# Training step of two attention and two GLU layers: one GLU slope product fused on VectorE, a scale delayed by one chunk, and query and slope loaded apart in attention backward

## The chip, the cores and the metric

The kernel runs on one core of a Trainium2 chip. Its engines are TensorE (PE in the profile, with PEld for its weight loads), VectorE (DVE), ScalarE (ACT), GpSimd (POOL) and SyncE (SP, which mainly issues transfers). Each engine executes its own instructions in order; semaphores tie the engines together. The metric is the device time of one execution in microseconds (us), and the median over several runs is compared.

## The reference

The input x is 2048 tokens by 512 features, in bf16. Two kinds of layer are applied twice in turn, A, B, A, B, each to the layer norm of x and added to x. Then the gradients with respect to x and all weights are taken for a given output gradient.

```python
def A(x, wqkv, wo):                      # 32 heads of 16 features
    q, k, v = heads(x @ wqkv)
    phi = lambda t: where(t > 0, t + 1, exp(t)) + 1e-6
    pq, pk = phi(q), phi(k)
    kv, z = einsum("bhsd,bhse->bhde", pk, v), einsum("bhsd->bhd", pk)
    num = einsum("bhqd,bhde->bhqe", pq, kv)
    den = einsum("bhqd,bhd->bhq", pq, z)[..., None] + 1e-6
    return merge(num / den) @ wo

def B(x, w_gate, w_up, w_down):          # 512 -> 1376 -> 512
    return (sigmoid(x @ w_gate) * (x @ w_up)) @ w_down

x = x + A(layernorm(x)); x = x + B(layernorm(x))
x = x + A(layernorm(x)); x = x + B(layernorm(x))
# outputs: x, and d(x . grad_out) / d(A_x, wqkv, wo, w_gate, w_up, w_down)
```

The B layers are called GLU layers here. Both A layers share their weights, and so do both B layers.

## The kernel before, in words

The layers are numbered 0 to 3; 0 and 2 are attention, 1 and 3 GLU. The 2048 tokens are cut into NBLK = 4 blocks of SB = 512, each of NB = 4 tiles of 128; the 512 features into NDC = 4 chunks, and the 1376 GLU features into NFC = 11 chunks of 128 (the last overlaps). The kernel is written with a tile framework: tiles come from pools with a fixed number of buffers, the framework sets the waits and moves instructions within each engine's order by its own estimate, so the order of the source is only approximately the order on an engine. Parts of different layers are generators that are stepped in turn, which interleaves their work.

`glu` (L635) makes one chunk of one block: four matmuls each for g and u into two PSUM banks. With t = tanh(-g/2), ScalarE leaves t in place of g (L647) and writes 1 - t into half 0 of the tile sd (L648); VectorE makes hh = (1 - t) u / 2 (L649), the activated value; ScalarE writes 1 + t into half 1 (L650), and GpSimd multiplies that by hh (L651). Half 1 is then the slope that the gradient of g needs, half 0 that of u.

The time line of the profiled execution:

- to 112 us: attention layer 0 and the first block of GLU layer 1;
- 112 to 215 us: forward of GLU layer 1 (`b_fwd`), interleaved with the second half of layer 0 (L532, L535, L546: den, its reciprocal, the output products). Each block's `down` (L675) multiplies hh by the down weights and adds to x (L428), and then asks for the layer norm of that block for layer 2 (`nxt.need`): per two tiles two ACT squares (L299), POOL's L301 and L302, two DVE operations L304, and a DMA transpose (L307); per block a store (L310). hh and sd are stored by SP for the backward.
- 215 to 524 us: attention layer 2, then forward and backward of GLU layer 3 in one pass (`b_both`, from 267 us). For each chunk: `glu`, then dhh = the down weights' transpose by the gradient (four matmuls, ACT L732), then VectorE's one multiplication of both slopes by dhh (L733, "scale"), in place, and the stores of the result: in block 0 by `store_dd`, afterwards by a DMA transpose in `turn_dd`. In its first block the second half of layer 2 runs between. `dh_b` (L790) makes the gradient of the block's normed input. The transposed gate and up weights wgT and wuT are loaded during this stage by `load_b_bwd`: a big transposing transfer (L418), a small one (L419), and a GpSimd memset of the unused rows (L420).
- 524 to 574 us: first backward half of attention layer 2 (`a_bwd1`); the same for layer 0 from 766 to 813 us. Per block SP loads `qr` (query and slope together, 1024 KB, tag "sh" with 2 buffers) and qn (512 KB). Per chunk: dq (PE L180, copied by ACT L1005), u = dq times query (DVE L1007), a sum over heads (PE L977, t_ps), w (DVE L979, tile w_t with 2 buffers), dqT = w times slope (POOL L980), and a product for the normaliser (DVE L981). `k.fill.step` inserts matmuls of weight gradients between.
- 574 to 640 us second half of that layer; 640 to 766 us the backward of GLU layer 1 (`b_bwd`, L868, L885); 766 to 880 us attention layer 0; from 880 us the weight gradients (L1199, L1217).

In the forward 8 PSUM banks serve the tag "bank", in the backward 4.

Of the kernel before, what the change touches and what calls it, by code (L numbers as in the profile page):

```python
# [7 lines left out]
BF16 = mybir.dt.bfloat16  # L8
F32 = mybir.dt.float32
ACT = mybir.ActivationFunctionType  # L10
ALU = mybir.AluOpType
# [620 lines left out]
                yield True  # L632


def glu(k, hT, fc):  # L635

    nc = k.nc
    g_ps = k.ps.tile([P, SB], F32, name="g_ps", tag="bank")
    mm4(k, g_ps[:], lambda c: k.wg[:, c, FC0[fc]:FC0[fc] + P], lambda c: hT[:, :, c, :])
    u_ps = k.ps.tile([P, SB], F32, name="u_ps", tag="bank")  # L640
    mm4(k, u_ps[:], lambda c: k.wu[:, c, FC0[fc]:FC0[fc] + P], lambda c: hT[:, :, c, :])
    hh = k.p_hh.tile([P, SB], BF16, name="hh_t")
    if k.n_sd % 2 == 0:
        k.sd2 = k.p_sd.tile([P, 2, 2, SB], BF16, name="sd_t", tag="sd")
    sd = k.sd2[:, k.n_sd % 2]
    k.n_sd += 1
    nc.scalar.activation(g_ps[:], g_ps[:], ACT.Tanh, scale=-0.5)  # L647
    nc.scalar.activation(sd[:, 0, :], g_ps[:], ACT.Identity, bias=k.onef[:], scale=-1.0)  # L648
    nc.vector.scalar_tensor_tensor(hh[:], sd[:, 0, :], 0.5, u_ps[:], ALU.mult, ALU.mult)  # L649
    nc.scalar.activation(sd[:, 1, :], g_ps[:], ACT.Identity, bias=k.onef[:])  # L650
    nc.gpsimd.tensor_tensor(sd[:, 1, :], sd[:, 1, :], hh[:], ALU.mult)  # L651
    return hh, sd


# [5 lines left out]
def b_fwd(k, l, ln, nxt):  # L660
    nc, sv = k.nc, k.sv[l]
    hhs, late = {}, []

    def store():

        b, fc, hh, sd = late.pop()
        store_hh(k, sv, b, fc, hh, nc.sync)
        nc.sync.dma_start(out=sv["sd"][b, fc], in_=sd.rearrange("p a b -> p (a b)"))

    def down(b):  # L670
        ys = [k.ps.tile([P, D], F32, name="y_ps", tag="bank") for _ in range(NB)]
        for fcs in (range(NFC - 1), (NFC - 1,)):
            for j in range(NB):
                for fc in fcs:
                    nc.tensor.matmul(ys[j][:], lhsT=hhs[b][fc][:, rows(j)], rhs=k.wd[:, fc, :],  # L675
                                     start=(fc == 0), stop=(fc == NFC - 1))
        for j in range(NB):
            add_x(k, b * NB + j, ys[j])
        nxt.need(b * NB + NB - 1)

    for b in range(NBLK):
        hhs[b] = []
        if b:
            down(b - 1)
        for fc in range(NFC):
            hh, sd = glu(k, ln.hT[b], fc)
            hhs[b].append(hh)
            if late:
                store()
            late.append((b, fc, hh, sd))  # L690
            yield b, fc
    store()
    down(NBLK - 1)


def last_grads(k, b):
# [7 lines left out]
def b_both(k, l, ln, ctx):  # L704

    nc, sv = k.nc, k.sv[l]
    pool = lambda name, bufs: ctx.enter_context(k.tc.tile_pool(name=name, bufs=bufs))
    hhs, dds, gns, gTs = {}, {}, k.gns, k.gTs
    k.n_t, k.fused = 2, lambda st: True

    def down(b):
        for j in range(NB):
            st = b * NB + j
            y_ps = k.ps.tile([P, D], F32, name="y_ps", tag="bank")
            mm4(k, y_ps[:], lambda fc: hhs[b][fc][:, rows(j)], lambda fc: k.wd[:, fc, :], NFC)
            if j % 2 == 0:
                ost = k.p_o.tile([P, 2, D], BF16, name="o0_t")
            nc.vector.tensor_tensor(ost[:, j % 2, :], y_ps[:], k.xs[st][:], ALU.add)
            if j % 2:
                k.st.dma_start(out=by_tile(k.out0, st - 1, 2), in_=ost[:])  # L720

    for b in range(NBLK):
        ln.need(b * NB + NB - 1)
        hhs[b], dds[b] = [], []
        if b == 1:
            k.p_ln, k.p_o, k.p_nat = pool("ln3", 2), pool("o3", 2), pool("nat", 2)
        for fc in range(NFC):
# [5 lines left out]
            k.last_mul = nc.vector.tensor_tensor(dd, dhh[:].unsqueeze(1).to_broadcast([P, 2, SB]), dd, ALU.mult)  # L733
            hhs[b].append(hh)
            dds[b].append(dd)
            if b:
                turn_dd(k, sv, b, fc, dd)
            else:
                store_dd(k, sv, b, fc, dd, nc.sync)
            store_hh(k, sv, b, fc, hh, k.st)  # L740
            if fc == 1 and b:
                down(b - 1)
                dh_b(k, l, b - 1, dds[b - 1], ln.h[b - 1], gns[b - 1])
            if fc == 3 and b + 1 < NBLK:
                last_grads(k, b + 1)
                if b:
                    ln.need((b + 2) * NB - 1)
            if b == NBLK - 1 and fc == 5:
                k.early = a_grads(k, 0)
            yield b, fc  # L750
    b = NBLK - 1
    down(b)
    dh_b(k, l, b, dds[b], ln.h[b], gns[b])
    flush_nat(k)


def turn_dd(k, sv, b, fc, dd):

    i, f = divmod(fc, 4)
    p0 = FDUP if fc == NFC - 1 else 0  # L760
    if f == 0:
        k.nat = k.p_nat.tile([P, 2, NB, D], BF16, name="nat_t")
    k.nc.sync.dma_start_transpose(
        out=k.nat[:, :, :, f * P - p0:(f + 1) * P - p0].rearrange("p a j f -> p (a j) f"),
        in_=dd.rearrange("p a s -> p (a s)"))
    if f == 1:
        flush_nat(k)
    if f == 3 or fc == NFC - 1:
        w = SETS[i][1]
        k.nats.append((sv["ddN"][b, i, :, :, :, 0:w], k.nat[:, :, :, 0:w]))  # L770
# [190 lines left out]
def a_bwd1(k, l, big, ph1, p_dq):  # L961
# [2 lines left out]
    nc.sync.dma_start(out=flat(MT), in_=sv["MT"][:])  # L964
    dzp = big.tile([P, NDC, NBLK], F32, name="dzp")
    CT_ps = [k.ps2.tile([P, D], F32, name="CT_ps", tag="dwbank") for _ in range(NDC)]
    late, gs, dqTs = [], [k.early], []

    def sums(b, g_t, qn):
        for jc in range(NDC):  # L970
# [1 line left out]
                nc.tensor.matmul(CT_ps[jc][:], lhsT=g_t[:, j, jc * P:(jc + 1) * P], rhs=qn[:, :, j, :],  # L972
                                 start=(b == 0 and j == 0), stop=(b == NBLK - 1 and j == NB - 1))

    def soft(b, dc, dq, u_t, qp, rp, dqT):
        t_ps = k.ps.tile([P, SB], F32, name="t_ps", tag="bank")
        nc.tensor.matmul(t_ps[:], lhsT=k.bdmask[:], rhs=u_t[:], start=True, stop=True)  # L977
        w_t = ph1.tile([P, SB], BF16, name="w_t")
        nc.vector.scalar_tensor_tensor(w_t[:], t_ps[:], A["nz"][:, dc:dc + 1], dq[:], ALU.mult, ALU.add)  # L979
        nc.gpsimd.tensor_tensor(dqT[:, dc, :], w_t[:], rp[:, dc, :], ALU.mult)  # L980
        nc.vector.scalar_tensor_tensor(u_t[:], t_ps[:], -1.0, qp[:, dc, :], ALU.mult, ALU.mult,  # L981
                                       accum_out=dzp[:, dc, b:b + 1])
        if dc == NDC - 1:
            k.st.dma_start(out=by_chunk(sv["dqT"], b), in_=dqT[:])

    k.fill.step(12)
    for b in range(NBLK):
        g_t, gT = gs[b]
        qr = k.p_sh.tile([P, 2, NDC, SB], BF16, name="qr_l", tag="sh")
        qp, rp = qr[:, 0], qr[:, 1]  # L990
        nc.sync.dma_start(out=flat(qr), in_=sv["qr"][b])
        qn = k.p_h.tile([P, NDC, NB, P], BF16, name="qn_l", tag="h_t")
        nc.sync.dma_start(out=flat(qn), in_=sv["qn"][b])
        if b == 1 and l == 2:
            nc.sync.dma_start_transpose(out=k.woT[:], in_=k.w_in["wo"])
            nc.sync.dma_start_transpose(out=k.wqkvT[:], in_=k.w_in["wqkv"])
        if b == NBLK - 1 and l == 2:
            held(k, k.mark, nc.sync.dma_start_transpose(out=k.wdT[:], in_=k.w_in["wd"]))
        dqT = p_dq.tile([P, NDC, SB], BF16, name="dqT_t")
        dqTs.append(dqT)  # L1000
        for dc in range(NDC):
            ps = k.ps.tile([P, SB], F32, name="dq_ps", tag="bank")
            mm4(k, ps[:], lambda c: MT[:, c, dc * P:(dc + 1) * P], lambda c: gT[:, :, c, :])
            dq = ph1.tile([P, SB], BF16, name="dq_sb", bufs=3)
            k.mark = nc.scalar.copy(dq[:], ps[:])  # L1005
            u_t = ph1.tile([P, SB], BF16, name="u_t", bufs=3)
            nc.vector.tensor_tensor(u_t[:], dq[:], qp[:, dc, :], ALU.mult)  # L1007
            late.append((b, dc, dq, u_t, qp, rp, dqT))
            k.fill.step(2)
            if len(late) > 2:  # L1010
                soft(*late.pop(0))
            if dc in (0, 2) and b + 1 < NBLK:
                g = a_grads(k, b + 1, dc // 2)
                if dc:
                    gs.append(g)
        sums(b, g_t, qn)
    while late:
        soft(*late.pop(0))
# [236 lines left out]
```

## Time and profile before

| | |
|---|---|
| median of 13 runs | 1136.6 us |
| lowest and highest | 1131.16 and 1143.16 us |
| the profiled execution | 1131.92 us, of which the span 1130.0 us |
| mean granted TensorE clock | 0.994 |
| PE busy | 1079.6 us (96%) |
| DVE, ACT, POOL busy | 528.1, 487.5, 325.9 us |
| loads of query and slope | 8 of 1024 KB, 7.2 us from issue to landing |
| loads of qn | 8 of 512 KB, 4.8 us |

How to read the lines of the profile: a group line names the source line, engine, operation, output and inputs, shape and count; then the busy time and mean length of one, and the idle time just before, with what ended it. A line of the time line gives start and length in us, and in square brackets how long the engine stood idle before and which instruction released it. The rows by stretch give for each engine its busy time and number of instructions, then the granted TensorE clock (1.00 is full speed), the mean busy share of the 16 DMA engines (waiting transfers can take it over 1), and GB/s.

### The profile page before, as it was taken

The page shows a single profiled execution, that of the slowest core. Times are in us where ns is not written, and L with a number is a line of the kernel's source. Part 1 is how long each engine was busy: PE and PEld are TensorE (multiplying, and loading weights), DVE is VectorE, ACT ScalarE, POOL GpSimd, SP SyncE. Part 2 cuts the span into 40 slices and gives each one's busy share as a digit, 9 for nine tenths or more (in the row PEclk, how much of TensorE's full clock was granted, in tenths as well). Part 3 has the DMA queues.
Part 4 walks back from the last instruction along what each step waited for, and adds up shares of the span by engine and source line. Part 5 has one row for each costly group of instructions (what it writes and reads, how often), then busy time and mean ns, then how long its engine had stood idle before and what let it go on. Part 6 is the DMA issues. An engine that isn't in the chain of part 4 may idle for free.

```text
span 1130.0 us, 15668 instructions
## 1 busy us (share of the span) xinstructions
PE 1079.6 (96%) x5624; PEld 509.2 (45%) x5624; DVE 528.1 (47%) x983; ACT 487.5 (43%) x1002; POOL 325.9 (29%) x427
## 2 busy tenths in 40 slices
PE   6989999998899999999899999999999999999898
PEld 3444444444334444444444444444444444464343
DVE  7685755667734445434657624556667100000100
ACT  3476877547635546453425533335436100000011
POOL 5424655303632526141442200003513200001110
PEclk9999999999999999999999999999999999999899
DMA  9977988679993939399995898859973797689995
GB/s 263 270 226 238 261 235 246 189 181 239 289 224 85 247 82 238 90 248 279 231 333 167 222 272 232 242 169 310 346 198 101 181 281 175 145 184 256 251 226 133
DMA packets 376558, 248.12 MB, mean 220 GB/s; under 512 B 288785, under 2 KB 341041, under 8 KB 374689
## 3 DMA queue, kind: packets, MB, share of 16 engines
q1 hardware_dynamic: 361424, 197.73, 70.3%
q0 software_dynamic: 15056, 49.39, 12.7%
q8 instruction: 44, 0.72, 0.3%
q14 instruction: 34, 0.27, 0.1%
HBM read 74.48 MB, written 102.20 MB: 156 GB/s over the span
## 4 chain that ended last, share of the span: by engine, by line
PE 26%; issue 20%; POOL 4%; DMA 3%; DVE 2%; ACT 1%; POOLq 0%; DVEq 0%; ACTq 0%
PE dh_ps L885 7%; PE dhh_ps L180 3%; PE fill_ps L236 3%; PE dw_ps L1199 2%; PE CT_ps L972 2%; PE dh_ps L790 2%; PE dq_ps L180 2%; PE dh_ps L1107 2%; PE dh_ps L1046 2%; DMA qr_l<-sv_qr 1%; POOL out_dram L1127 1%; PE dpk_ps L180 1%; POOL x L865 1%; PE y_ps L180 1%; DMA hf_t<-sv_hhT 1%
## 5 line engine op out<-in xcount | busy, mean ns | idle before, releaser
L1199 PE MATMUL dw_ps<-set_t,h_all 128*128 128x512 bf16 (+1 forms) x1024 | 204.8, 362 | 2.0 <-ACT dw_new L1126 2.0
L1199 PEld LDWEIGHTS <-h_all 128*128 128x128 bf16 x1024 | 100.1, 98 | 106.0 <-issue 2.6
L651 POOL TENSOR_TENSOR sd_t<-sd_t,hh_t 128x512 bf16<-128x512 bf16 x88 | 106.6, 1220 | 120.0 <-DVE hh_t L649 89.2
L1126 ACT CAST dw_new<-dw_ps 128x512 bf16<-128x512 f32 (+1 forms) x40 | 19.8, 572 | 220.7 <-PE dw_ps L1199 156.2
L855 ACT ACTIVATE t_sb<-dh_ps,rstd 128x512 f32<-128x512 f32 x64 | 43.5, 680 | 131.6 <-PE dh_ps L790 94.9
L180 PE MATMUL g_ps<-hT_t,wg 128*128 128x512 bf16 x352 | 90.5, 379 | 6.9 <-DVE hh_t L649 3.7
L1223 DVE TENSOR_TENSOR dw_new<-dw_ps,part_l 128x512 bf16<-128x512 f32 (+1 forms) x11 | 7.2, 687 | 181.2 <-PE dw_ps L1217 168.5
L180 PE MATMUL u_ps<-hT_t,wu 128*128 128x512 bf16 x352 | 90.5, 379 | 0.6 <-DVE hh_t L649 0.6
L180 PE MATMUL dhh_ps<-gT_t,wdT 128*128 128x512 bf16 x352 | 90.3, 379 | 0.0
L885 PE MATMUL dh_ps<-wgT,dd_t 128*128 128x512 bf16 x176 | 66.7, 379 | 0.0
L885 PE MATMUL dh_ps<-wuT,dd_t 128*128 128x512 bf16 x176 | 66.7, 379 | 0.0
L649 DVE SCALAR_TENSOR_TENSOR hh_t<-sd_t,u_ps 128x512 bf16<-128x512 bf16 x88 | 59.2, 678 | 14.1 <-ACT sd_t L648 13.5
L1127 POOL DMA_DIRECT2D out_dram<-dw_new x36 | 19.3, 541 | 151.6 <-ACT dw_new L1126 150.2
L648 ACT ACTIVATE sd_t<-g_ps,onef 128x512 bf16<-128x512 f32 x88 | 60.8, 690 | 2.5
L650 ACT ACTIVATE sd_t<-g_ps,onef 128x512 bf16<-128x512 f32 x88 | 60.6, 688 | 0.0
L733 DVE TENSOR_TENSOR sd_t<-dhh_t,sd_t 128x1024 bf16<-128x1024 bf16 x44 | 30.4, 692 | 61.4 <-POOL sd_t L651 60.0
L908 DVE TENSOR_TENSOR dd_t<-dhh_t,sh_t 128x1024 bf16<-128x1024 bf16 x44 | 29.9, 689 | 58.6 <-ACT dhh_t L906 48.3
L647 ACT ACTIVATE g_ps<-g_ps 128x512 f32<-128x512 f32 x88 | 52.4, 602 | 8.8 <-PE g_ps L180 8.7
L180 PEld LDWEIGHTS <-wg 128*128 128x128 bf16 x352 | 33.9, 98 | 47.1 <-issue 8.8
L180 PEld LDWEIGHTS <-wu 128*128 128x128 bf16 x352 | 34.4, 98 | 42.3 <-issue 0.9
L885 PEld LDWEIGHTS <-dd_t 128*128 128x128 bf16 x352 | 34.4, 98 | 41.5
L790 PEld LDWEIGHTS <-sd_t 128*128 128x128 bf16 x352 | 34.4, 98 | 41.6
(172 smaller groups left out, 1863.3 us busy)
## 6 DMA issues: line engine op xcount, KB each, us to landing
sv_sd<-sd_t SPq DMA_DIRECT2D x44, 256.0 KB, 3.0
sv_ddT<-dd_t SPq DMA_DIRECT2D x40, 256.0 KB, 4.4
sv_h<-h_t POOLq DMA_DIRECT2D x16, 512.0 KB, 5.3
sv_qr<-pe_t POOLq DMA_DIRECT2D x16, 512.0 KB, 5.4
qr_l<-sv_qr SPq DMA_DIRECT2D x8, 1024.0 KB, 7.2
sh_t<-sv_sd SPq DMA_DIRECT2D x8, 1024.0 KB, 6.8
h_all<-sv_h SPq DMA_DIRECT2D x16, 512.0 KB, 6.1
sv_ddN<-nat_t SPq DMA_DIRECT2D x6, 1024.0 KB, 4.3
```

Of the source, the lines that this page charges most:

```text
L180: i = k.nc.tensor.matmul(out, lhsT=lhs(c), rhs=rhs(c), start=(c == 0), stop=(c == n - 1))
L236: nc.tensor.matmul(ps[0:w, :], lhsT=t[:, st, 0:w], rhs=self.g[st // NB][:, st % NB, :], start=(st == 0), stop=(st == NST - 1))
L647: nc.scalar.activation(g_ps[:], g_ps[:], ACT.Tanh, scale=-0.5)
L648: nc.scalar.activation(sd[:, 0, :], g_ps[:], ACT.Identity, bias=k.onef[:], scale=-1.0)
L649: nc.vector.scalar_tensor_tensor(hh[:], sd[:, 0, :], 0.5, u_ps[:], ALU.mult, ALU.mult)
L650: nc.scalar.activation(sd[:, 1, :], g_ps[:], ACT.Identity, bias=k.onef[:])
L651: nc.gpsimd.tensor_tensor(sd[:, 1, :], sd[:, 1, :], hh[:], ALU.mult)
L790: k.nc.tensor.matmul(dh_ps[:], lhsT=dds[fc][:, a, rows(j)], rhs=(k.wuT, k.wgT)[a][:, fc, :], start=(i == 0), stop=(i == 2 * NFC - 1))
L855: nc.scalar.activation(t_sb[:], dh_ps, ACT.Identity, scale=rstd, accum_out=c1[:])
L885: nc.tensor.matmul(acc[b][j][:], lhsT=dd[:, a, rows(j)], rhs=(k.wuT, k.wgT)[a][:, fc, :], start=(fc == 0 and a == 0), stop=(fc == NFC - 1 ...
L1127: (eng or k.st).dma_start(out=k.outs[nm][rs, cs], in_=new[0:r, 0:w])
L1199: k.nc.tensor.matmul(ps[ic][:, 0:w], lhsT=h_m[:, ic * P:(ic + 1) * P], rhs=t_m, start=(m == 0), stop=(m == n - 1))
```

## The change

It has three parts, and one move.

1. In layer 1, for the odd chunks of every block (5 of 11), half 1 of sd is made in one VectorE operation from t in PSUM and hh: (t + 1) hh. ACT's L650 and POOL's L651 remain for the even chunks and for layer 3. The layer norm of a finished block is asked for two tiles each behind chunks 2 and 4 of the following block, the last block's after its `down`.
2. In layer 3 the scale of a chunk, with its stores, is issued a chunk later, after the next chunk's ACT L732.
3. In attention backward the query half and the slope half are loaded by two transfers. Two blocks' queries share one tile of tag "sh", so all four have room; the slope is loaded into the dqT tile and GpSimd multiplies in place. The loads of block b+1, qn too, are issued in block b behind its third chunk.

In the built order of the engines this also moves some instructions that the diff does not name. On POOL the slopes and hhT stores of chunks 9 and 10 of block 0 in layer 3 stand ahead of the memset of wuT (before, both memsets stood between the slopes of chunks 8 and 9). On SP the order was small wuT, small wgT, a ddT store, big wuT, big wgT; it becomes big wuT, small wuT, big wgT, small wgT, all behind two ddT stores. In attention layer 2 the first slope load stands behind the transposes of the attention weights (wo, wqkv); the three later ones follow between other loads. SP issues 381 rows of instructions in place of 388.

```diff
-def glu(k, hT, fc):
+def glu(k, hT, fc, fused=False):
...
     nc.vector.scalar_tensor_tensor(hh[:], sd[:, 0, :], 0.5, u_ps[:], ALU.mult, ALU.mult)
-    nc.scalar.activation(sd[:, 1, :], g_ps[:], ACT.Identity, bias=k.onef[:])
-    nc.gpsimd.tensor_tensor(sd[:, 1, :], sd[:, 1, :], hh[:], ALU.mult)
+    if fused:
+        nc.vector.scalar_tensor_tensor(sd[:, 1, :], g_ps[:], 1.0, hh[:], ALU.add, ALU.mult)
+    else:
+        nc.scalar.activation(sd[:, 1, :], g_ps[:], ACT.Identity, bias=k.onef[:])
+        nc.gpsimd.tensor_tensor(sd[:, 1, :], sd[:, 1, :], hh[:], ALU.mult)
...
# b_fwd
-        nxt.need(b * NB + NB - 1)
...
-            hh, sd = glu(k, ln.hT[b], fc)
+            hh, sd = glu(k, ln.hT[b], fc, fc % 2 == 1)
...
+            if b and fc in (2, 4):
+                nxt.need((b - 1) * NB + (1 if fc == 2 else 3))
             yield b, fc
     store()
     down(NBLK - 1)
+    nxt.need(NST - 1)
...
# b_both
+    def scale(b, fc, dhh, dd):
+        k.last_mul = nc.vector.tensor_tensor(dd, dhh[:].unsqueeze(1).to_broadcast([P, 2, SB]), dd, ALU.mult)
+        if b:
+            turn_dd(k, sv, b, fc, dd)
+        else:
+            store_dd(k, sv, b, fc, dd, nc.sync)
...
             nc.scalar.mul(dhh[:], ps[:], 0.5)
-            k.last_mul = nc.vector.tensor_tensor(dd, dhh[:].unsqueeze(1).to_broadcast([P, 2, SB]), dd, ALU.mult)
+            if late:
+                scale(*late.pop())
+            late.append((b, fc, dhh, dd))
             hhs[b].append(hh)
             dds[b].append(dd)
-            if b:
-                turn_dd(k, sv, b, fc, dd)
-            else:
-                store_dd(k, sv, b, fc, dd, nc.sync)
...
+    scale(*late.pop())
...
# a_bwd1
+    def loads(b):
+        if b % 2 == 0:
+            qps.append(k.p_sh.tile([P, 2, NDC, SB], BF16, name="qp_l", tag="sh"))
+        dqTs.append(p_dq.tile([P, NDC, SB], BF16, name="dqT_t"))
+        half = NDC * SB
+        nc.sync.dma_start(out=flat(qps[-1][:, b % 2]), in_=sv["qr"][b][:, 0:half])
+        nc.sync.dma_start(out=flat(dqTs[b]), in_=sv["qr"][b][:, half:2 * half])
+        qns.append(k.p_h.tile([P, NDC, NB, P], BF16, name="qn_l", tag="h_t"))
+        nc.sync.dma_start(out=flat(qns[b]), in_=sv["qn"][b])
...
-        nc.gpsimd.tensor_tensor(dqT[:, dc, :], w_t[:], rp[:, dc, :], ALU.mult)
+        nc.gpsimd.tensor_tensor(dqT[:, dc, :], w_t[:], dqT[:, dc, :], ALU.mult)
...
+    loads(0)
     k.fill.step(12)
     for b in range(NBLK):
         g_t, gT = gs[b]
-        qr = k.p_sh.tile([P, 2, NDC, SB], BF16, name="qr_l", tag="sh")
-        qp, rp = qr[:, 0], qr[:, 1]
-        nc.sync.dma_start(out=flat(qr), in_=sv["qr"][b])
-        qn = k.p_h.tile([P, NDC, NB, P], BF16, name="qn_l", tag="h_t")
-        nc.sync.dma_start(out=flat(qn), in_=sv["qn"][b])
+        qp, dqT, qn = qps[b // 2][:, b % 2], dqTs[b], qns[b]
...
                 if dc:
                     gs.append(g)
+                    loads(b + 1)
```

More of the change, by code (lines that the diff above doesn't have):

```diff
@@ L720, in down @@
                 k.st.dma_start(out=by_tile(k.out0, st - 1, 2), in_=ost[:])
+    def scale(b, fc, dhh, dd):
[4 more added lines that the diff above has]
+            store_dd(k, sv, b, fc, dd, nc.sync)
+    late = []
     for b in range(NBLK):
@@ L966, in a_bwd1 @@
     CT_ps = [k.ps2.tile([P, D], F32, name="CT_ps", tag="dwbank") for _ in range(NDC)]
-    late, gs, dqTs = [], [k.early], []
+    late, gs, dqTs, qps, qns = [], [k.early], [], [], []
+    def loads(b):
[7 more added lines that the diff above has]
+        nc.sync.dma_start(out=flat(qns[b]), in_=sv["qn"][b])
     def sums(b, g_t, qn):
@@ L973, in sums, with soft @@
                                  start=(b == 0 and j == 0), stop=(b == NBLK - 1 and j == NB - 1))
-    def soft(b, dc, dq, u_t, qp, rp, dqT):
+    def soft(b, dc, dq, u_t, qp, dqT):
         t_ps = k.ps.tile([P, SB], F32, name="t_ps", tag="bank")
@@ L998, in a_bwd1 @@
             held(k, k.mark, nc.sync.dma_start_transpose(out=k.wdT[:], in_=k.w_in["wd"]))
-        dqT = p_dq.tile([P, NDC, SB], BF16, name="dqT_t")
-        dqTs.append(dqT)
         for dc in range(NDC):
@@ L1007, in a_bwd1 @@
             nc.vector.tensor_tensor(u_t[:], dq[:], qp[:, dc, :], ALU.mult)
-            late.append((b, dc, dq, u_t, qp, rp, dqT))
+            late.append((b, dc, dq, u_t, qp, dqT))
             k.fill.step(2)
```

## The prediction

> **What bounds the kernel now.** I read the busy shares first, then the groups and waits of the touched lines, then stretch by stretch the idle time ahead of TensorE (PE) instructions, each followed back.
>
> ```profile
> PE 1079.6 (96%) x5624; PEld 509.2 (45%) x5624; DVE 528.1 (47%) x983; ACT 487.5 (43%) x1002; POOL 325.9 (29%) x427
> ...
> L651 POOL TENSOR_TENSOR sd_t<-sd_t,hh_t 128x512 bf16<-128x512 bf16 x88 | 106.6, 1220 | 120.0 <-DVE hh_t L649 89.2
> ...
> L733 DVE TENSOR_TENSOR sd_t<-dhh_t,sd_t 128x1024 bf16<-128x1024 bf16 x44 | 30.4, 692 | 61.4 <-POOL sd_t L651 60.0
> ```
>
> PE is the bound: 1079.6 of 1130.0 us. Emptying another engine gains only where PE waits for it, so the 60.0 us of L733 are not a prize; PE's gaps are. In forward layer 1 (112 to 215 us):
>
> ```profile
> 114.37 1.00 DVE L304 TENSOR_SCALAR h_t<-x,ln_neg,rstd 128x512 bf16<-128x512 f32 x2 [2.08 <-POOL rstd L302]
> 115.29 0.68 DVE L649 SCALAR_TENSOR_TENSOR hh_t<-sd_t,u_ps 128x512 bf16<-128x512 bf16 x1
> 116.02 1.02 PE L180 MATMUL g_ps<-hT_t,wg 128*128 128x512 bf16 x4 [1.31 <-DVE hh_t L649]
> ...
> 152.13 1.02 PE L180 MATMUL g_ps<-hT_t,wg 128*128 128x512 bf16 x4 [1.31 <-DVE hh_t L649]
> ```
>
> VectorE (DVE) stands 2.08 us at the layer norm of the next layer, which comes all at once after `down`, and hh, which frees PE's banks, is queued behind it. Layer 3, block 0:
>
> ```profile
> 302.91 0.69 DVE L733 TENSOR_TENSOR sd_t<-dhh_t,sd_t 128x1024 bf16<-128x1024 bf16 x1 [1.04 <-POOL sd_t L651]
> 303.52 0.68 DVE L535 TENSOR_TENSOR pe_t<-pe_t,rd_t 128x1024 bf16<-128x1024 bf16 x1
> ...
> 304.26 0.61 PE L180 MATMUL y_ps<-M_t,pe_t 128*128 128x512 bf16 x2 [2.62 <-DVE pe_t L535]
> ...
> 321.48 0.51 POOL L420 MEMSET wgT<- 32x512 bf16 x1 [0.96 <-DMA wgT<-in_B_w_gate_dram]
> 321.97 1.14 POOL L651 TENSOR_TENSOR sd_t<-sd_t,hh_t 128x512 bf16<-128x512 bf16 x1
> ...
> 323.15 0.69 DVE L733 TENSOR_TENSOR sd_t<-dhh_t,sd_t 128x1024 bf16<-128x1024 bf16 x1 [8.18 <-POOL sd_t L651]
> 323.76 0.68 DVE L649 SCALAR_TENSOR_TENSOR hh_t<-sd_t,u_ps 128x512 bf16<-128x512 bf16 x1
> ...
> 324.49 1.01 PE L180 MATMUL y_ps<-wd,hh_t 128*128 128x512 bf16 x2 [2.78 <-DVE hh_t L649]
> ```
>
> Twice L733 waits for the slope on POOL, and what PE needs (L535, then hh) is behind it in DVE's order; the second time POOL itself sat behind memsets that wait for DMAs. Attention backward, layers 2 and 0:
>
> ```profile
> 563.28 0.42 DVE L1007 TENSOR_TENSOR u_t<-dq_sb,qr_l 128x512 bf16<-128x512 bf16 x1 [4.17 <-DMA qr_l<-sv_qr]
> ...
> 565.11 1.02 PE L180 MATMUL dq_ps<-gaT_t,MT_l 128*128 128x512 bf16 x4 [2.99 <-ACT dq_sb L1005]
> ...
> 803.97 0.42 DVE L1007 TENSOR_TENSOR u_t<-dq_sb,qr_l 128x512 bf16<-128x512 bf16 x1 [3.58 <-DMA qr_l<-sv_qr]
> ...
> 805.80 1.02 PE L180 MATMUL dq_ps<-gaT_t,MT_l 128*128 128x512 bf16 x4 [0.73 <-ACT dq_sb L1005]
> ```
>
> Here the 1 MB load lands after PE has got there. Behind these stages PE is nearly full to the end (stalls of 3.67, 0.74 and 1.26 us, untouched), so a gain in PE reaches the end.
>
> **The change part by part.**
>
> *Layer 1, odd chunks.* 20 calls lose an ACT copy (L650, 0.688 us) and a POOL product (1.220) and gain one DVE operation on a PSUM operand; nearest row L649, 0.678: DVE +13.6, ACT −13.8, POOL −24.4 us. DVE is 62.9 us busy of the 100 from 112, so 76 after; the fullest ten microseconds (152 to 162) hold 9.46. The layer norm of the finished block moves behind chunks 2 and 4 of the next, so its four ACT squares (about 3.6 us) no longer precede the first hh. Stalls of that kind: 1.31+0.52+0.21+1.31, and 1.00 before L535 at 155.01: 4.35. I take 4.0, since a fused operation ahead of hh puts 0.68 back; ends −5.6 (each of eight hh beside a moved layer norm comes 0.7 late) and 4.35. With the layer norm move, per two tiles, POOL's L301 and L302 (0.19 and 0.71), DVE's two L304, one transpose on SP (L307), and per block the 512 KB store L310 on POOL's queue. They pass SP's sd and hhT stores and POOL's even-chunk slopes, which only feed stores; the output serves the next layer, and the last block's still follows the last `down`. Cover: layer 2 starts at 215, tens of us after the third block's.
>
> *Layer 3, delayed scale.* L733 goes one chunk later, behind the next hh, when its slope is 2.6 us old. L535 at 291 (1.33) and 304 (2.62) no longer stand behind a wait: 3.95. In blocks 1 to 3 the loop hh, slope, scale, hh runs at 2.61 us against PE's 12 × 0.2157 = 2.59, with stalls of 0.59, 0.74 and 0.35; it opens: 1.7. The ddT stores and their transposes on SP also come a chunk later, behind `last_grads`' loads where they stood ahead; nobody uses them before `dh_b`. The dhh tile has two buffers and is held a chunk longer, so ACT's L732 waits for the scale of two chunks before (7.9 us in 15 waits today, under the old order); behind it is the next tanh. The scale then runs right after the hh of the chunk, before L732 comes: nothing, or 0.3 for each of 44 (13 us) if DVE falls behind.
>
> *POOL and SP around the memsets.* In the built order slopes and stores of chunks 9 and 10 go ahead of the wuT memset; the 2.78 stall goes, and with it the slow clock behind it (the 0.83 row below): 27 matmuls at some 51 ns extra, 1.4. On SP the big wuT transpose moves ahead of both small ones, the big wgT stays behind them, past two late ddT stores. Before, it was issued at 326.79, landed 9.9 later (336.7) and was needed at 337.83. Everything earlier runs about 8.1 sooner, so PE asks at 329.5; with the same landings it lands about 331.6: a new stall of 2.0 (0 to 4). Sum 2.2.
>
> *Attention loads.* 1 MB per block becomes two 512 KB loads, the slope into dqT, a block ahead. That removes 2.99 (layer 2) and 1.07+0.73 (layer 0), and the slow clock after 565:
>
> ```profile
> 320.00:330.00 10.00, 7.22 (x27) 2.89 (x26) 3.87 (x6) 2.95 (x5) 6.18 (x9) 0.83 1.11 208
> ...
> 566.00:568.00 2.00, 2.00 (x7) 0.71 (x6) 1.90 (x5) 0.58 (x1) 1.70 (x2) 0.61 0.70 155
> 568.00:570.00 2.00, 2.00 (x6) 0.73 (x5) 0.71 (x3) 0.58 (x1) 1.23 (x2) 0.54 1.28 290
> ```
>
> (the number after the five engines is the granted clock). The last two rows lose 2×(1−0.61)+2×(1−0.54) = 1.7. The Trainium skill ("TensorE: Matmul & The Clock Gate", Part 1: The HAM clock gate) has the clock halved only after an idle window of about 3.4 us; by that, gaps of 2.78 and 2.99 cost no clock, and the sum is 3.1 smaller. The trace decides: both gaps were followed by a lower clock, though the 2.62 one was not.
>
> New cost: in layer 2 the first slope load may not start before a buffer is freed at 527.05, and on SP stands behind the weight transposes, which end at 533.6. A load of its size issued at 533.68 landed in 6.0, so the slope is there at 539.7; POOL's first product was at 533.2 before. POOL's wait holds w_t (two buffers) on DVE, then the t_ps banks, then PE: landing minus 537.86, or 1.9 (0 to 4). The skill ("DMA: Bandwidth & Descriptors", Bandwidth) asks for transfers of at least 1 MiB, which speaks against the split; its 0.95 us for 64 KB and 6.15 for 1 MB give an estimate of 3.4 for a half, landing at 537.1, no delay. I keep the row: the DMA share was over 1 there. By rows halves are dearer too (4.8 each against 7.2), but a block ahead hides that; without that cover it is 2.4 per block on eight blocks, 19 us. In layer 0 the slope waits for the last L885 (765.3), before the stage. Net: layer 2 2.99+1.7−1.9 = 2.8; layer 0 1.8.
>
> **Sum:** 4.0 + 3.95 + 1.7 + 2.2 + 2.8 + 1.8 = 16.4 (the sum with every new cost at nothing is 20.7). The profiled execution is 1131.92, 1130.0 of it the span; it lies 4.7 below the median of 1136.6. So 1115.5 for that execution, and 1136.6 − 16 = 1120.6, say 1121, for the median.
>
> **The rivals.**
> 1. *Half is given back to transfers.* The stage has full DMA stretches (1.08 in 275 to 300, 1.11 in 320 to 330); wgT and the first slope land 4 us later than estimated, costing 8. For: SP serves in order and everything is pulled forward against the same DMA. Against: fewer bytes move at those places. 16.4−8: about 1128.
> 2. *DVE becomes the bound of layer 1.* 76 us of work at these durations; but beside a POOL product one L304 took 1.36 (at 116.42), alone 0.50. If such stretching reaches the average DVE operation there, the stage is DVE's: break-even with the other gains (12.4) is 100+12.4 us, a factor of 1.47; at 1.55 it is 118, so +18−12.4: 1142, slower. Against: the change takes 24.4 us of POOL away there.
> 3. *The changed order does not take the waits off PE.* In chunks 0 to 2 of block 0 the built order of DVE is unchanged; L546 (1.22) and L428 may hold hh as L733 did, and the layer norm between chunks stall hh just as well. Gains of layers 1 and 3 fail, the attention's 4.6 less a 4-us clash at wgT remain: 1136.
>
> **How the numbers follow.** Forecast 0.62, rival 1 0.16, rival 3 0.09, rival 2 0.13. About 0.3% (3.4 us) is what a measurement of this kernel can tell from no change. Forecast and rival 1 are faster: 0.78; rival 3 is the same: 0.09; rival 2 slower: 0.13. The range starts at 20.7 us of gain and some scatter of the runs below it (1113) and goes to rival 3 (1136).
>
> **What would show it.** Right: no PE gap above 0.5 us at the first hh of blocks 1 and 2 of layer 1; L733's wait for L651 falls from 60.0 to under 15; no 2.6-us gap before y_ps in layer 3 and no qr_l wait of L1007; no clock under 0.8 in 320 to 330. A wait of POOL L980 for the dqT load and one of PE for wgT should appear, 2 us each. Wrong: DVE over 90% in 112 to 212 with PE waiting for hh, or PE waiting over 5 us for wgT or dq.

## The result: 10 us faster, and the profile after

The changed kernel took 1126.67 us (median of 11 runs, 1122.69 to 1131.12) against 1136.71 (48 runs): ratio 0.9912, 95% interval 0.9894 to 0.993, so 8 to 12 us less. The profiled execution was 1125.40 us, 1123.7 of it the span; that is 6.3 less than the span before. Lines of the changed kernel have numbers of their own: L651 there is the fused operation, L654 the slope on POOL, L728 the scale, L745 dhh, L1003 the product with the attention's slope, L802 `dh_b`.

From the page of the changed kernel, the busy time and the two groups:

```profile
PE 1078.9 (96%) x5624; PEld 509.4 (45%) x5624; DVE 538.8 (48%) x1003; ACT 477.0 (42%) x982; POOL 303.2 (27%) x407
...
L654 POOL TENSOR_TENSOR sd_t<-sd_t,hh_t 128x512 bf16<-128x512 bf16 x68 | 83.6, 1230 | 153.9 <-DVE hh_t L649 110.4
...
L728 DVE TENSOR_TENSOR sd_t<-dhh_t,sd_t 128x1024 bf16<-128x1024 bf16 x44 | 30.4, 691 | 60.4 <-POOL sd_t L654 59.0
```

PE's own work did not change; 22.7 us left POOL and 10.5 ScalarE. But the scale still waits 59.0 us for the slope, where the prediction wanted under 15: the first sign that a step was not carried out. The waits of the changed kernel (total, times, longest) show two behind transfers. The one for the slope (L1003) is new; the memset of wuT waited before, too, 7.4 us, which the profile puts down to PE:

```profile
DVE sd_t L728 <- POOL sd_t L654: 59.0, 38, 10.6
...
POOL wuT L420 <- DMA wuT<-in_B_w_up_dram: 9.8, 1, 9.8
...
POOL dqT_t L1003 <- DMA dqT_t<-sv_qr: 7.6, 1, 7.6
```

PE's gaps in the changed kernel, from its time line:

```profile
137.29 0.39 PE L678 MATMUL y_ps<-wd,hh_t 128*128 128x512 bf16 x1 [0.75 <-DVE hh_t L649]
138.36 7.73 PE L678 MATMUL y_ps<-wd,hh_t 128*128 128x512 bf16 x35 [0.68 <-DVE hh_t L649]
...
299.54 0.61 PE L180 MATMUL y_ps<-M_t,pe_t 128*128 128x512 bf16 x2 [1.93 <-DVE pe_t L535]
331.05 2.53 PE L802 MATMUL dh_ps<-wgT,sd_t 128*128 128x512 bf16 x11 [1.56 <-DMA wgT<-in_B_w_gate_dram]
364.81 1.02 PE L180 MATMUL u_ps<-hT_t,wu 128*128 128x512 bf16 x4 [0.58 <-DVE hh_t L649]
370.05 1.02 PE L180 MATMUL g_ps<-hT_t,wg 128*128 128x512 bf16 x4 [0.73 <-DVE hh_t L649]
...
536.09 0.48 PE L1000 MATMUL t_ps<-u_t,bdmask 128*128 128x512 bf16 x1 [1.99 <-DVE u_t L1004]
...
827.26 3.63 PE L180 MATMUL dpk_ps<-haT_l,Wp_t 128*128 128x512 bf16 x16 [1.06 <-DMA haT_l<-sv_hT]
```

Gone are the two gaps of 1.31 in layer 1, the 2.78 at 324 us, the 2.99 at 565 and the two of layer 0. Left is 1.93 of the 2.62. New are the waits for wgT (1.56), for the first slope (1.99 at 536) and for haT (1.06). Those of blocks 1 to 3 of layer 3 (0.58, 0.73) have not moved at all. The clock of 320 to 330 us, 0.83 before, is 1.00.

Cutting the span at the same PE instructions in every trace shows where the time went. (The "fill" matmuls are those that `k.fill.step` inserts.) The cuts are the first g of layer 1; the second L532 burst (about 250 us); the first g of layer 3; the first fill matmul behind it (525); the dpk matmul at 614; the fill matmul at 773; the dq matmul at 806. Times in us; "old" are the traces in which that part of the kernel is as before (seven where no number is given), "new" those in which it is as changed and otherwise as in the changed kernel (for the last three rows all seven with the loads apart); the start and the 17.1 us between the second cut and the third are left out:

| stage | before | changed | old, mean (range) | new, mean (range) |
|---|---|---|---|---|
| layer 1 | 173.7 | 171.2 | 173.5 (173.3 to 173.7, four traces) | 171.2 (171.2 to 171.3) |
| layer 3 | 257.1 | 252.1 | 256.7 (253.6 to 259.9, six traces) | 252.2 (251.3 to 254.1) |
| attention 2 to dpk | 89.1 | 89.0 | 90.8 (89.1 to 94.5) | 89.1 (86.4 to 90.8) |
| dpk to layer 0's fill | 159.3 | 159.9 | 159.1 (158.8 to 159.5) | 160.0 (159.0 to 162.5) |
| attention 0 | 32.7 | 31.0 | 34.6 (32.5 to 36.9) | 31.0 (31.0 to 31.1) |
| from there to the end | 324.2 | 325.9 | 324.0 (323.4 to 324.9) | 326.4 (323.9 to 332.2) |

The means give 2.3 + 4.5 + 1.7 − 0.9 + 3.6 − 2.4 = 8.8, near the 10 of the medians. Three of the seven "new" traces in the last rows hold the first slope's mend that is described below; without them the two losses are 1.2 and 0.8, and the sum is 10.1. The pair of single traces gives 6.3, mostly because the trace before happened to have short attention stages (1.9 and 1.7 under the means of layers 0 and 2).

### The profile page after: what moved, and what is told of

The parts are those of the page before. It is cut to its first block, busy times and chain, and to the rows that moved or that the text cites. A ratio compares the mean times of both kernels' runs of the same rounds, so it can differ in the third digit from the quotient of the medians.

```text
span 1123.7 us, 15629 instructions
## 1 busy us (share of the span) xinstructions
PE 1078.9 (96%) x5624; PEld 509.4 (45%) x5624; DVE 538.8 (48%) x1003; ACT 477.0 (42%) x982; POOL 303.2 (27%) x407
## 4 chain that ended last, share of the span: by engine, by line
PE 26%; issue 21%; POOL 4%; DMA 3%; ACT 2%; DVE 1%; POOLq 0%; ACTq 0%; DVEq 0%
PE dh_ps L897 6%; PE dhh_ps L180 3%; PE fill_ps L236 2%; PE dw_ps L1218 2%; PE CT_ps L995 2%; PE dq_ps L180 2%; PE dh_ps L802 2%; PE dh_ps L1065 2%; PE dh_ps L1126 1%; POOL x L877 1%; POOL out_dram L1146 1%; PE dpk_ps L180 1%; PE y_ps L180 1%; PE t_ps L1000 1%; DMA hf_t<-sv_hhT 1%
## 5 line engine op out<-in xcount | busy, mean ns | idle before, releaser
L654 POOL TENSOR_TENSOR sd_t<-sd_t,hh_t 128x512 bf16<-128x512 bf16 x68 | 83.6, 1230 | 153.9 <-DVE hh_t L649 110.4
L180 PE MATMUL g_ps<-hT_t,wg 128*128 128x512 bf16 x352 | 90.8, 379 | 4.2 <-ACT hT_t L322 2.3
L649 DVE SCALAR_TENSOR_TENSOR hh_t<-sd_t,u_ps 128x512 bf16<-128x512 bf16 x88 | 59.5, 679 | 10.5 <-ACT sd_t L648 9.8
L648 ACT ACTIVATE sd_t<-g_ps,onef 128x512 bf16<-128x512 f32 x88 | 60.4, 689 | 2.8
L728 DVE TENSOR_TENSOR sd_t<-dhh_t,sd_t 128x1024 bf16<-128x1024 bf16 x44 | 30.4, 691 | 60.4 <-POOL sd_t L654 59.0
L802 PEld LDWEIGHTS <-sd_t 128*128 128x128 bf16 x352 | 34.4, 98 | 43.3 <-issue 1.8
L180 PEld LDWEIGHTS <-wdT 128*128 128x128 bf16 x352 | 34.4, 98 | 42.0 <-issue 0.9
```

The source lines that it names most:

```text
L180: i = k.nc.tensor.matmul(out, lhsT=lhs(c), rhs=rhs(c), start=(c == 0), stop=(c == n - 1))
L802: k.nc.tensor.matmul(dh_ps[:], lhsT=dds[fc][:, a, rows(j)], rhs=(k.wuT, k.wgT)[a][:, fc, :], start=(i == 0), stop=(i == 2 * NFC - 1))
```

## The experiments

All ratios are to the kernel before, run on the same chip. In the single-trace readings the stage lengths of the table are used. A trace is that of one execution, and need not be a middling one: that of the kernel with the order edge was the fastest of six runs, that of the layer norm's move alone the slowest of twelve, that of the last version the slowest of four. So stages are compared, and not spans.

### Each part alone

Part 1 alone, as in the diff of the change (fused slope for odd chunks of layer 1, layer norm moved).

> The kernel before with part 1 alone (fused slope for odd chunks of layer 1, layer norm moved). Theory: PE's gaps at the first hh of blocks 1 and 2 (1.31 each) go, the small ones at 138 and 155 stay; the trace of the changed kernel has PE 1.85 us earlier at 250 us after starting 0.69 later, so 2.5 us from this part: about 1134.2 against 1136.7, ratio 0.998. Rival (VectorE becomes the bound): ratio 1.00 or above, with new PE waits for hh in 112 to 212 us. If the prediction's term was right and the trace of the changed kernel is off by chance: 4.0 us, 0.9965.

1134.01 us, ratio 0.9973 (0.9957 to 0.999). Layer 1 took 171.3 us, the 1.31 gaps are gone, and no other wait of their size came: part 1 is worth 2.3 us by the means of the table.

Part 2 alone (`late` and `scale` in `b_both`).

> The kernel before with part 2 alone (scale one chunk later in the source of layer 3). In the built order only 3 of the 44 scales stand behind the next chunk's hh, all in block 0. Theory: block 0 gains 5.0 us as in the changed kernel (the 2.78 and 1.33 gaps and the slow clock go, 2.62 becomes about 1.9, a new wait for wgT of 1.6 appears), blocks 1 to 3 keep their gaps of 0.59, 0.74 and 0.35: about 1131.7, ratio 0.9956. Rival (the delay itself works through the whole layer): gaps in blocks 1 to 3 gone, 6.7 us, ratio 0.994.

1131.43 us, ratio 0.9962 (0.9946 to 0.9977); layer 3 took 251.3 us. The gaps of blocks 1 to 3 were there unchanged (0.62, 0.74, 0.38), and the wait for wgT was 0.57. So part 2 gains 4.3 us by the total and 4.5 by the means of the stage, in block 0 and its `down`.

Part 3 alone (`a_bwd1`).

> The kernel before with part 3 alone (query and slope loaded apart). Theory: layer 2 exchanges a gap of 2.99 and its slow clock (1.7) for one of 2.0 at the first slope and a slow clock behind that (1.7), net 1 us or less; layer 0 gains 1.6 and gives some back at a later load: 1 to 2.5 us in all, ratio 0.998 to 0.999. Rival (prediction's term): 4.6 us, ratio 0.996. Rival (the split only moves waits to loads behind it): 1.000.

1134.82 us, ratio 0.9987 (0.9966 to 1.0009). Layer 2 showed the exchange (a gap of 2.55 at 544 us for the 2.99 at 565), layer 0 took 31.05 us, and a wait of 1.35 for haT appeared at 836. By the total alone it can't be told from no change. The three ratios multiply to 0.9973 × 0.9962 × 0.9987 = 0.9922, inside the interval of the whole (0.9894 to 0.993): the parts add up.

The same load in layer 0 is late by very different amounts. Of the kernel with part 1 alone, VectorE's time line:

```profile
795.79 0.42 DVE L1012 TENSOR_TENSOR u_t<-dq_sb,qr_l 128x512 bf16<-128x512 bf16 x1 [3.67 <-DMA qr_l<-sv_qr]
```

PE stood 3.66 us behind it there, against 1.07 and 0.73 in the trace before. With the loads a block ahead the stage is 31.0 in all seven traces. What part 3 took away is mostly this scatter.

### Was the scale late at all?

In the built order of the changed kernel, only 3 of 44 scales stand behind the next chunk's hh on VectorE, all three in block 0; the scheduler put the other 41 back where they were. The time line of the changed kernel in block 1 shows the old loop:

```profile
363.47 0.69 DVE L728 TENSOR_TENSOR sd_t<-dhh_t,sd_t 128x1024 bf16<-128x1024 bf16 x1 [2.95 <-POOL sd_t L654]
364.08 0.68 DVE L649 SCALAR_TENSOR_TENSOR hh_t<-sd_t,u_ps 128x512 bf16<-128x512 bf16 x1
```

The changed kernel with an order edge between the two, 40 scales:

```diff
+    k.last_hh = nc.vector.scalar_tensor_tensor(hh[:], sd[:, 0, :], 0.5, u_ps[:], ALU.mult, ALU.mult)
...
     def scale(b, fc, dhh, dd):
         k.last_mul = nc.vector.tensor_tensor(dd, dhh[:].unsqueeze(1).to_broadcast([P, 2, SB]), dd, ALU.mult)
+        if fc < NFC - 1:
+            after(k, k.last_mul, k.last_hh)
```

> The changed kernel with an order edge that makes each scale of chunks 0 to 9 stand behind the next chunk's hh on VectorE, so that the delay written in the source happens in the built order (40 of 44 chunks, against 3). Theory: the prediction's mechanism was right and only not carried out: the gaps in blocks 1 to 3 (0.58, 0.73, 0.33 with the loop at 2.62 us) go, the wait of the scale for the slope falls from 59 us to under 5, time 1.7 us or more under the changed kernel, about 1125. Rival: another loop of the same length (the two dhh buffers, ScalarE waiting for the scale) holds the pace: same time as the changed kernel, 1126.7. Rival on the other side: the later scale delays stores and transposes so that dh_b waits for dd: 1128 or more.

1124.05 us, ratio 0.9894 (0.9866 to 0.9923); span 1116.7. From its waits and its time line:

```profile
DVE sd_t L728 <- POOL sd_t L654: 14.3, 8, 7.4
```

```profile
368.60 0.69 DVE L649 SCALAR_TENSOR_TENSOR hh_t<-sd_t,u_ps 128x512 bf16<-128x512 bf16 x1 [0.73 <-ACT sd_t L648]
369.20 0.68 DVE L728 TENSOR_TENSOR sd_t<-dhh_t,sd_t 128x1024 bf16<-128x1024 bf16 x1
```

The scale now starts the moment hh is done, without waiting, and hh waits for ScalarE's input alone. The wait of 59.0 is 14.3, not the under 5 expected: 7.4 of it is one wait. No PE gap is left in blocks 1 to 3, and layer 3 took 250.0 us, 249.6 on the average of the three traces with the edge, 2.7 less than without.

Cut at the first g of each block, the traces without the edge (four) and with it (three, one with the fused slope in block 0 as well) agree among themselves to 0.15 us: block 0 takes 46.5 without and 46.0 with it, block 1 apart from its wait for wgT 58.8 and 57.4, block 2 57.6 and 57.0, block 3 with the last `dh_b` 86.8 and 86.5. So the order alone gives 0.5 in block 0 and 2.3 in blocks 1 to 3. The rest is transfers: the wait for wgT was 0.8 shorter on the average, and the first fill matmul behind the layer stood 1.0 longer, no longer for ScalarE (0.87 to 1.06) but for its load (1.55 to 2.11):

```profile
515.66 2.75 PE L236 MATMUL fill_ps<-gf_t,hf_t 128*128 128x512 bf16 x12 [2.10 <-DMA hf_t<-sv_hhT]
```

The mechanism was right; the diff did not carry it out. The two intervals (0.9866 to 0.9923 and 0.9894 to 0.993) overlap, so for the 2.7 the stage is the evidence, not the total.

### Which half of part 1?

The layer norm's move alone:

```diff
-        nxt.need(b * NB + NB - 1)
...
+            if b and fc in (2, 4):
+                nxt.need((b - 1) * NB + (1 if fc == 2 else 3))
...
+    nxt.need(NST - 1)
```

> The kernel before with the layer norm's move alone (no fused slope). Theory: the move takes the four squares and the wait for POOL's rstd away from the first hh, so the two gaps of 1.31 at 116 and 152 go: about 2.5 us, the whole gain of part 1, ratio 0.998. Rival (the fused slope gave it, by emptying POOL, which also makes rstd): gaps stay, ratio 1.000. Rival on the other side (beside the slope products on POOL the moved layer norm is stretched and delays hh): new waits for hh, above 1.000.

1138.16 us, ratio 1.0023 (0.9998 to 1.0048): my theory was wrong. Layer 1 took 175.9 us, 2.4 more than without the edit. Its time line on VectorE, and on PE:

```profile
129.14 1.00 DVE L304 TENSOR_SCALAR h_t<-x,ln_neg,rstd 128x512 bf16<-128x512 f32 x2 [2.42 <-POOL rstd L302]
```

```profile
140.64 0.39 PE L675 MATMUL y_ps<-wd,hh_t 128*128 128x512 bf16 x1 [2.17 <-DVE hh_t L649]
...
172.63 1.02 PE L180 MATMUL g_ps<-hT_t,wg 128*128 128x512 bf16 x4 [1.52 <-ACT sd_t L650]
```

The layer norm still holds VectorE, now between chunks, with add_x (L428) and hh queued behind it, and one gap is ScalarE's.

The fused slope alone:

```diff
-            hh, sd = glu(k, ln.hT[b], fc)
+            hh, sd = glu(k, ln.hT[b], fc, fc % 2 == 1)
```

> The kernel before with the fused slope alone (20 of 44 chunks of layer 1, layer norm where it was). Theory: 24 us off POOL and 14 off ScalarE, 14 more on VectorE, none of it where PE waits: the 1.31 gaps stay, ratio 1.000, at most 0.7 us either way. Rival: with part of the work off ScalarE and POOL the squares and rstd come sooner and the gaps shrink: 0.998. Rival (VectorE bound): a gap or two of 0.7 more, 1.001.

1130.62 us, ratio 0.9962 (0.994 to 0.9983). Layer 1 took 172.8, 0.7 less; both 1.31 gaps stayed:

```profile
116.09 1.02 PE L180 MATMUL g_ps<-hT_t,wg 128*128 128x512 bf16 x4 [1.31 <-DVE hh_t L649]
...
151.31 1.02 PE L180 MATMUL g_ps<-hT_t,wg 128*128 128x512 bf16 x4 [1.31 <-DVE hh_t L649]
```

The rest of its gain lies in layer 3 (253.6 us, the shortest of the "old" traces, with 0.40 in place of the 2.78 gap), which this edit does not touch; I put that down to where its transfers fell, but it is not shown. The total is that of twelve runs, so it is more than the luck of one trace, and what it is stays open. By the totals the move adds nothing to the fused slope (0.9973 with it, 0.9962 without); that it pays is read from layer 1 alone, 171.3 against 172.8. The halves of layer 1 do not add: +2.4 and −0.7 alone, −2.3 together. The move pays only when the fused operation has made room. On which engine? The next kernel has the layer norm moved, and the odd chunks' product on VectorE from the sd that ScalarE still writes, which relieves POOL alone:

```diff
-    nc.gpsimd.tensor_tensor(sd[:, 1, :], sd[:, 1, :], hh[:], ALU.mult)
+    (nc.vector if fused else nc.gpsimd).tensor_tensor(sd[:, 1, :], sd[:, 1, :], hh[:], ALU.mult)
```

> The kernel before with the layer norm moved and, for odd chunks of layer 1, the slope product on VectorE from the sd that ScalarE still writes: POOL is relieved as by the fused operation, ScalarE is not. The layer norm alone stretched layer 1 (from its first g to the second L532 burst) from 173.7 to 175.9 us, both together shortened it to 171.2. Theory: POOL is what made the moved layer norm wait (rstd stood behind a slope product): about 171.5 here as well. Rival: ScalarE, whose squares stand among tanh and two copies per chunk: about 175, POOL's relief alone does nothing. If both count: 173 to 174. Total time against before: 0.998 by the theory, 1.001 by the rival.

1139.55 us, ratio 1.0022 (1.0002 to 1.0042), layer 1 177.0 us: relieving POOL alone does nothing. The stretch from 112 to 215 us of this kernel and of part 1 alone (busy time of PE, PEld, DVE, ACT, POOL):

```profile
112.00:215.00 103.00, 96.12 (x478) 43.61 (x476) 67.35 (x126) 77.84 (x162) 39.12 (x48) 1.00 0.79 236
```

```profile
112.00:215.00 103.00, 100.34 (x498) 46.10 (x504) 69.13 (x134) 71.84 (x152) 38.11 (x48) 1.00 0.85 243
```

POOL is relieved alike (39.1 and 38.1, from 54.8) and VectorE is about as loaded; ScalarE differs, 77.8 against 71.8. VectorE did not stand for the copy in its new product (0.1 us at most before each of the 20). And the largest gap is ScalarE's, behind the very copy that the fused operation removes:

```profile
173.84 1.02 PE L180 MATMUL g_ps<-hT_t,wg 128*128 128x512 bf16 x4 [1.67 <-ACT sd_t L650]
```

So it is the copy of 0.69 us on ScalarE, and not the product of 1.22 on POOL, that had to go. One thing is not separated: the two kernels' built order on VectorE differs as well (all sixteen of the layer norm's L304 stand in pairs here, six stand alone in part 1).

### Block 0 of layer 3: the memsets

The kernel before, with only the two memsets on POOL behind the first slope of block 1, SP as before:

```diff
-    nc.gpsimd.memset(t[0:FDUP, NFC - 1, :], 0.0)
+    k.blank = getattr(k, "blank", []) + [t]
...
+            if b == 1 and fc == 0:
+                for t in k.blank:
+                    after(k, nc.gpsimd.memset(t[0:FDUP, NFC - 1, :], 0.0), k.slope)
...
```

> The kernel before with POOL's two memsets (wuT, wgT) moved behind the slope of the first chunk of block 1, SP's order of the transposes as before. Theory: the 2.78 gap at 324 us (or what stands for it) goes, but PE then comes sooner to dh_b and waits for wgT, whose load goes out no sooner: 2 to 3 us of wait at about 335; net 1 to 2 us, ratio 0.9985, so part 2's gain needs SP's new order as well. Rival (the memsets alone are the cause): 3.5 to 4.2 us, ratio 0.9965. Rival: no gain, 1.000, if the gap is set by the transposes in any order.

1137.21 us, ratio 1.0006 (0.9986 to 1.0026). The gap at 324 is gone and stands at wgT:

```profile
337.26 3.15 PE L794 MATMUL dh_ps<-wgT,sd_t 128*128 128x512 bf16 x7 [3.73 <-DMA wgT<-in_B_w_gate_dram]
```

The memsets were the near cause of the 2.78 gap and worth nothing on their own: PE comes to `dh_b` sooner, and wgT no sooner. Part 2 also changed SP's order; that the gain needs it is argued. The landing of the loads can do it as well: in the trace of the fused slope alone, with the old order on both engines, PE stood 0.40 at `down` and not at all for wgT.

### The first slope

In the changed kernel, on SP, POOL, and in the clock (the number after the five engines):

```profile
519.75 7.28 SPq L1016 DMA_TRANSPOSE wqkvT<-in_A_wqkv_dram  x1
527.19 0.95 SPq L988 DMA_DIRECT2D dqT_t<-sv_qr  x2
```

```profile
532.89 3.56 POOL L1003 TENSOR_TENSOR dqT_t<-w_t,dqT_t 128x512 bf16<-128x512 bf16 x3 [7.57 <-DMA dqT_t<-sv_qr]
```

```profile
536.00:538.00 2.00, 1.91 (x5) 0.70 (x5) 1.36 (x5) 0.00 (x0) 0.93 (x2) 0.56 1.37 278
538.00:540.00 2.00, 2.00 (x10) 0.89 (x9) 1.13 (x4) 0.58 (x1) 1.57 (x2) 0.59 0.81 180
```

The slope goes out behind the transpose, POOL starts on it 5.7 us later, and PE's 1.99 is followed by a clock of 0.56 and 0.59, 1.7 us more. The changed kernel with that transpose held back to the third block:

```diff
-            nc.sync.dma_start_transpose(out=k.wqkvT[:], in_=k.w_in["wqkv"])
+        if b == 2 and l == 2:
+            held(k, k.mark, nc.sync.dma_start_transpose(out=k.wqkvT[:], in_=k.w_in["wqkv"]))
```

> The changed kernel with the transposing load of wqkv in attention layer 2 held back to the third block, so that on SP the first slope load goes out behind the wo transpose only. Theory: POOL's first product no longer waits 7.6 us, PE's gap of 2.0 at 536 us and the slow clock behind it (1.7) go: 2 to 3.7 us under the changed kernel, about 1124. Rival (the slope is not what PE waits for, or the transfers are saturated there and land as late): gap of 1 us or more remains, 1126.7. Rival (the transpose held back is late for its own use at about 590 us, or crowds haT): new gap there, 1126 to 1128.

1124.02 us, ratio 0.9884 (0.9849 to 0.9918). On SP the slope now leaves ahead of the transpose:

```profile
521.50 1.25 SPq L988 DMA_DIRECT2D dqT_t<-sv_qr  x2
```

The gap of 2.0 with its slow clock is gone: the stretch from the first fill matmul (519 us) to the dq matmul at 557, at 559 in the changed kernel, took 37.6 us against 41.2. But most of it was given back before dpk. PE and VectorE of this kernel:

```profile
591.55 1.89 PE L236 MATMUL fill_ps<-gf_t,hf_t 128*128 128x512 bf16 x7 [3.00 <-DVE dkT_t L1079]
```

```profile
586.20 0.69 DVE L1072 TENSOR_SCALAR dph_t<-pkT_l 128x2048 bf16<-128x2048 bf16 x1 [7.11 <-DMA pkT_l<-sv_pkT]
```

Counted from the fill, PE was 3.7 us sooner than in the changed kernel and pkT landed 1.4 sooner (66.8 against 68.3); the same PE gap was 0.74 there. To dpk the stage is 87.5 against 89.0: both the theory and its second rival were partly right. But this gap scatters (0.6 to 2.0 in the traces with the loads apart and no mend here, 1.6 to 3.2 in six of the seven old ones), and the two later traces with this mend took 89.0 and 89.1, so a gain of the whole stage is not shown.

### Again, both mends, and one thing more

The changed kernel once more:

> The changed kernel once more, for a second trace of it and as the reference for the other runs of this call. Expected about 1126.7, ratio 0.991. The gaps set by VectorE's order (1.9 at 299, 0.58 and 0.73 at 365 to 370) return unchanged; those behind a transfer (wgT, the first slope, pkT, haT, the hhT set at 1047) differ by 1 to 3 us from the first trace, and their sum makes most of the scatter between runs.

1126.27 us, ratio 0.9921 (0.9884 to 0.9959). Its trace repeats VectorE's gaps to 0.02 us (1.92, 0.58, 0.73) while wgT's is 0.81 (1.56 before), the first slope's 2.32 (1.99), dkT's 1.86 (0.74), haT's 1.94 (1.06), as expected. Not expected were two gaps of 1.06 and 1.04 in layer 1's backward, behind ScalarE's dhh, which the first trace did not have.

The order edge and the slope ahead of the transpose are the two mends. Both together:

> The changed kernel with both mends: scale really a chunk late, and the first slope load ahead of the wqkv transpose. Theory: the two act in different stages and add up but for the pkT wait at about 590 us: 1.7 to 2.6 and 1.4 to 2.6 us under the changed kernel, 1121.5 to 1123, ratio about 0.987. Rival (the transfers of layer 2's second half set the pace, and what comes sooner waits there): no better than either mend alone, 1124.

1123.46 us (4 runs), ratio 0.9869 (0.984 to 0.9897). Layer 3 took 248.8, the first stretch of layer 2 37.6 again; then 2.74 at dkT and 2.31 at haT. Better than the changed kernel by the point value, but not told apart from it or from one mend alone.

The fused slope also for the odd chunks of block 0 of layer 3, on top of both mends (`glu(k, ln.hT[b], fc, b == 0 and fc % 2 == 1)`):

> The version with both mends, and the fused slope also for the odd chunks of block 0 of layer 3, where VectorE shares the time with the attention's second half and the gap of 1.9 at 299 us is left (L546 took 2.17 and L535 1.63 there beside a POOL product, 1.22 and 0.68 elsewhere). Theory: fewer POOL products, less stretching, the 1.9 gap under 0.8: 1 us faster than with both mends. Rival (0.68 more on VectorE per odd chunk in a stage where it is over 80% busy): new gaps before y_ps of 1 to 2 us, 1 to 2 us slower.

1121.56 us (4 runs), ratio 0.9847 (0.981 to 0.9885), the lowest. Its interval is the only one below the changed kernel's (0.9894 to 0.993), but it touches that of the changed kernel run again beside it (0.9884 to 0.9959), its four runs go from 1118 to 1129 us, and the medians alone (1121.56 to 1135.55) give 0.988. Its trace doesn't credit the last edit with it: the 1.92 gap went to 1.08 and two others came,

```profile
286.55 0.82 PE L180 MATMUL y_ps<-M_t,pe_t 128*128 128x512 bf16 x3 [0.80 <-DVE pe_t L535]
288.28 1.25 PE L180 MATMUL y_ps<-M_t,pe_t 128*128 128x512 bf16 x5 [0.92 <-DVE pe_t L535]
...
299.71 0.61 PE L180 MATMUL y_ps<-M_t,pe_t 128*128 128x512 bf16 x2 [1.08 <-DVE pe_t L535]
```

and layer 3 took 249.9, no less than with the mends. So theory and rival cancel in this stage; that the lower total is the mends' is likely, and not shown.

## Why the prediction was right, and where it was off

The direction, the bound (PE, and the named gaps) and the range held: 1126.7 lies in 1113 to 1136, but 5.7 above the 1121 named. The range was wide, with hardly any gain at its upper end, and rival 1's 1128 lies nearer than the 1121. Some terms were too large and one too small. Term by term, forecast against the stage means:

- *Layer 1, 4.0: measured 2.3.* The 1.31 gaps went as said. Mis-sized was what stays: 1.99 of the 4.35, where 0.35 was left over (0.75 and 0.68 ahead of `down`'s y_ps at 137 and 138, where 0.52 and 0.21 stood, and 0.56 of the 1.00 before L535). And the reason given was half of one: the forecast credited the layer norm's move and treated the copies taken off ScalarE as a number without a place. The move alone costs 2.4; with the room on ScalarE it pays. The low end of the term (−5.6) had the sign of the move alone.
- *Layer 3, 3.95 + 1.7 + 2.2 = 7.85: measured 4.5.* The step that failed is "L733 goes one chunk later". It was read from the source. Only 3 of 44 did in the built order, which I had read for block 0 (rival 3 names it for chunks 0 to 2) and not for the blocks where the 1.7 was claimed. With the edge, blocks 1 to 3 gain 2.3 by their order, where 1.7 was claimed, and the layer gains 7.2 in all against 7.85; that the sums come so near is partly luck, since waits for two transfers moved as well. In block 0 the 1.33 shrank to 0.24 and the 2.62 only to 1.93, since L546 and L535 there took 2.17 and 1.63; the wgT wait was 1.56 and 0.81 for the 2.0 (0.57 to 3.30 over the four traces).
- *Attention layer 2, 2.8: 1.7 by the means, 0.1 in the pair of traces.* The new gap was sized well (1.99 and 2.32 for 1.9). Left out was its slow clock, another 1.7: the same loss that the prediction had counted as a gain behind the gap it removed. The 1.7 of the means is uncertain: the ranges overlap, and PE's wait for dkT, for which the forecast had no term, was 0.2 in the trace before, 0.7 in the changed kernel and 1.6 to 3.2 in the six other old traces.
- *Attention layer 0, 1.8: 3.6.* One trace sized it, and that trace was among the short ones of seven.
- *Nothing was charged behind these stages; there went 0.9 and 2.4 (1.2 and 0.8 without the mends).* Before haT PE now waits 1.06 to 5.31 us with the loads apart, in seven traces of seven; with the old loads in one of seven (1.08). That is rival 1 (transfers give part of it back) at 2 to 3 us instead of 8, at places that it did not name; what else is in the 0.9 and 2.4 is open.

The first slope, 5.7 us from its issue to POOL's product, sides with the row of 6.0 against the estimate of 3.4 from the Trainium skill ("DMA: Bandwidth & Descriptors", Bandwidth). On the clock the trace again differs from "TensorE: Matmul & The Clock Gate" (Part 1: The HAM clock gate), which asks for an idle window of about 3.4 us: 1.99 us of idling were followed by 0.56 and 0.59, and 1.92 at 299 by none. No shorter threshold comes out of these traces: 3.08 us at 562 in part 1 alone and 3.00 at 591 with the slope ahead left the clock at 1.00. So the 1.4 and 1.7 that the forecast took for the slow clock could not be counted on. Rival 2 was wrong: VectorE went from 62.5 to 69.2 us of the 103 from 112 (its 62.9 for the first 100 of them reads 60.9 in the trace).

## What to carry to other kernels

A change of the source is not a change of the order: where a scheduler places instructions, count in the built order how many of the moved ones moved, stage by stage, and pin the rest with an edge. A gap behind a transfer read from one trace is one draw: what late loads cost attention layer 0 was 1.7 us in one trace and 5.9 in another, while the gaps that an engine's order sets came back to 0.02 us. When a load or an engine is made early, ask what the next transfer does: three times here a wait came up at the next load (wgT, haT, and the fill matmul's behind layer 3).

## What the runs showed of the hardware

A slow clock followed PE gaps as short as 1.99 us (536 us, clock 0.56 and 0.59 in the next 4 us), though not every gap of 2 to 3 us (2.62 at 304 before, 3.08 and 3.00 in two other traces were followed by 1.00). A DVE operation of 1.22 us (L546) took 2.17 beside a POOL product at 292 us in the changed kernel. Over all 14 traces, each of the 62 of 448 L535 and L546 that took over 1.15 times their usual length ran beside a POOL product for 0.4 us or more. Forty-five others did so too and were not longer, so the product goes with the stretching and is not the whole of it; taking the odd products away left the sum of the gaps as it was.
